# The stores of the attention's results move from SyncE's queue to ScalarE's

## The chip, the cores and the metric

The kernel runs on one core of a Trainium2 chip. The metric is the device time of one execution in microseconds (us); lower is better. The times shown are the median of several runs with the lowest and the highest of them. The profile comes from one further execution, whose own time is given beside its span.

Names used below: TensorE (PE) does matmuls and transposes, VectorE (DVE) and ScalarE (ACT) work on tiles elementwise, GpSimd (POOL) copies, and SyncE (SP) issues DMAs. An engine runs its instructions in order. A DMA is started by an instruction on an engine's queue, which takes a few tenths of a microsecond there; the transfer then goes on by itself, and whoever needs its data waits on a semaphore. In the profile, "SPq" stands for such issuing rows on SP.

## What is computed

Block-sparse attention for 4 batches and 8 heads, with 768 positions of 64 elements, followed by an MLP over the 3072 tokens:

```python
scores = scale * np.matmul(q, k.transpose(0, 1, 3, 2))
mask = np.abs(blk_i - blk_j) <= window          # blocks of 32 positions, window 1
mask = mask | (blk_i == 0) | (blk_j == 0) | (blk_i == n_blocks - 1) | (blk_j == n_blocks - 1)
# and 3 sampled key blocks for each query block
scores = np.where(mask, scores, -1000000000.0)
attn = np.exp(scores - np.max(scores, axis=-1, keepdims=True))
attn = attn / (np.sum(attn, axis=-1, keepdims=True) + 1e-09)
x = np.matmul(attn, v)        # then transposed and reshaped to 3072 x 512
h = x @ w_in                  # 512 x 2048, weights in float64
g = s * np.maximum(h, 0.0) ** 2 + b
out = g @ w_out               # 2048 x 512
```

## The kernel before

The attention is cut into 52 *slots*. A slot is a tile of 128 rows of queries for a few heads of one batch; most (kind s) see a static stretch of keys and their own sampled blocks, and the first and last blocks of a sequence, which see all keys, are slots of kind d (dense) and h. A slot has four *units* (a d slot two), and each unit is one score tile of up to 128×352.

The way of a slot through the engines, with the lines by which the profile names the steps:

- SP loads what is needed: keys `kt` (L490), queries `qr` (L500), values `v` (L508, L511, L514), and with `gather_v` (L653) the sampled value blocks `vg`. A gather is twelve or so single DMAs whose addresses come out of registers, so each has a register instruction beside it. POOL copies the sampled keys into `kg` (L670).
- PE computes the scores against static keys (L710, dense L724) and sampled keys (L736).
- DVE adds the mask and finds the row maximum (`maximum`, L751, one per unit); ACT computes the exponentials (L763, one per unit, with the row sum).
- PE transposes the exponentials (L787, 12 per slot); the four results `pt` are copied out of PSUM half by DVE (L791) and half by ACT (L793).
- PE multiplies them with the values: L832 (dense L821, kind h L826) for static ones, L846 for the gathered `vg`.
- DVE divides by the row sums (`x_scale`, L852), PE transposes the result (`x_transpose`, L858), ACT copies it from PSUM to an SBUF tile `xst` (`x_copy`, L863), and a DMA stores `xst` to `xd` in device memory (`spill`, L875): 128 KB for 44 of the slots, 64 KB for the 8 of kind d.

On PE these steps are interleaved: transposes of slot i, L858 of slot i−1, scores of slot i+2, then the value products of slot i. Tiles rotate in pools: `xst` has 4 buffers, `vg` 2 (each serves two batches), `v` 4, `raw` 3.

The MLP reads `xd` back (`xload`, L359), splits it into high and low parts (L372, L374), and multiplies with `w_in` (L401–L403) and `w_out` (L440–L442, and products of sums, L1193). The float64 weights arrive as integer words (`load`, L57, tiles `raw_i` and `raw_o`) and are decoded by DVE and ACT in nine steps (L75–L85) that begin during the second half of the attention.

What sets the order: the steps of the attention, the decoding and the first MLP units are handed as operations to a planner (class `Plan`, L99). Each has an engine, a cost in ns, a due time and its dependences. The planner simulates the five engines, takes the earliest operation that can start, and breaks ties by due time; the result is the order in which instructions are written. The engines then run that order, held only by semaphores. For a DMA on SP the planner also counts eight in flight (`QUEUE`): SP is taken as held until the DMA eight places earlier has landed. After 30 MLP units the rest is written in a fixed order by hand (L1242 on).

A DMA signals its landing on one of eight semaphores, which are taken in turn over all DMAs of the program; one that gets a semaphore again waits first until the DMA that had it last has landed.

In a spill's operation, `u` is the slot's first unit, and `T["XA"]` and `T["SPP"]` are offsets of the due time, −12 and −14 units:

```python
ac = op("a", 280 if kind == "d" else 390, u + T["XA"], lambda i=i: x_copy(i), [tr], alloc=[("xst", i)], use=[("o", i)])
```

Of the kernel before, what the change touches and what calls it, by code (L numbers as in the profile page):

```python
# [98 lines left out]
class Plan:  # L99
# [15 lines left out]
    def op(self, eng, cost, prio, fn, deps=(), alloc=(), use=(), order=(), nbytes=0, cols=0, late=0.0):  # L115


        o = Plan.Op()
        o.cost, o.prio, o.fn, o.nbytes, o.cols, o.late = cost if isinstance(cost, dict) else {eng: cost}, prio, fn, nbytes, cols, late
        o.pick = isinstance(cost, dict)  # L120
        o.deps, o.order, o.alloc = [d for d in deps if d], [d for d in order if d], alloc
        o.end, o.seq = None, len(self.ops)
        for k in (*alloc, *use):
            self.users.setdefault(k, []).append(o)
        self.ops.append(o)
        return o
# [76 lines left out]
def kernel(  # L203
# [16 lines left out]
    nc = tc.nc  # L220
# [238 lines left out]
    with ExitStack() as es:  # L459
# [400 lines left out]
        def x_copy(i):  # L860
            tr = tr_of.pop(i)
            xst_of[i] = xp.tile([P, 2, P], F32, tag="xst", name=f"xst{i}", bufs=4)[:, :tr.shape[1], :]
            nc.scalar.copy(xst_of[i], tr)  # L863

        def spill(i):
            kind, b, t, x = slots[i]
            hf, o = divmod(t * P, HALF)
            xst = xst_of.pop(i)
            if kind == "s":
                to = xd[b, hf, :, o // P, 2 * x:2 * x + 2]  # L870
            else:
                d0 = D * (kind == "d")
                to = xd[b, hf, :, o // P, 2 * x:2 * x + 2 * xst.shape[1], d0:d0 + D].rearrange("p (x a) q -> p x a q", a=2)
                xst = xst.rearrange("p x (a q) -> p x a q", a=2)
            nc.sync.dma_start(out=to, in_=xst)  # L875


        plan = Plan({"kraw": RB, "qr": QB, "v": 4, "kg": 4, "vg": 2, "B": NBANK,
# [2 lines left out]
        op = plan.op  # L881
        first, last = {}, {}
        for n, (i, j) in enumerate(units):
            kind, b, t, x = slots[i]
# [69 lines left out]
        spills, tensor, lqs = {}, {}, {}  # L954
# [3 lines left out]
        for i, (kind, b, t, x) in enumerate(slots):  # L958
            u, full, cost, col = unit_of[i], kind == "s", costs[kind], cols[kind]
            nu, ng, nk = (2, 2, 2) if kind == "d" else (4, 1, 2)  # L960
            qk = slots[i][:3]
            if qk not in lqs:
                for par in range(2):
                    pq = lqs[qk] = op("s", 450, u - T["QL"] + 0.1 * par, lambda qk=qk, par=par: load_q(qk, par), alloc=[] if par else [("qr", qk)],
                                      use=[("qr", qk)] if par else [], order=[pq], nbytes=131e3)
# [16 lines left out]
            if gd:  # L982
                o = op("p", cost[1], u, lambda i=i: scores_sampled(i), cols=col[1], deps=gd,
                       use=[("qr", qk), *gu, *(("B", ("s", *y)) for y in s_of)])
# [31 lines left out]
            if gd:  # L1016
                o = op("p", cost[4], u, lambda i=i: av_sampled(i), cols=col[4], deps=gvs[(b, t)],
                       use=[("o", i), ("vg", (b // 2, t)), *(("pt", (u + j, 0)) for j in range(nu))])
                a_ops.append(o)
            xc = op("v", 300 if kind == "d" else 430, u + T["XA"], lambda i=i: x_scale(i), [a_ops[-1], o_rc], alloc=[("xss", i)], use=[("o", i), ("rc", i)])  # L1020
            tr = op("p", 160 if kind == "d" else 230, u, lambda i=i: x_transpose(i), [xc], cols=256 if kind == "d" else 512, use=[("xss", i), ("o", i)])
            ac = op("a", 280 if kind == "d" else 390, u + T["XA"], lambda i=i: x_copy(i), [tr], alloc=[("xst", i)], use=[("o", i)])
            spills[i] = op("s", 450, u + T["SPP"], lambda i=i: spill(i), [ac], use=[("xst", i)], nbytes=66e3 if kind == "d" else 131e3)
            tensor[i] = s_ops, t_ops, a_ops, tr
        line = tensor[0][0] + tensor[1][0]
        for i in range(len(slots)):
# [20 lines left out]
        for g in range(2):  # L1047
            for c2 in range(2):
# [8 lines left out]
                for c in (2 * c2, 2 * c2 + 1):  # L1057
# [3 lines left out]
                                               use=[key], order=o_x)  # L1061
                    xs_ops[(g, c, 1)] = op("v", 450, N + T["XP"] + g * 16, lambda g=g, c=c: xsplit(g, c, 1), [h], use=[key], alloc=xkey[1], order=[xs_ops[(g, 0, 1)]] if c else [])
        wdone = {}
        for k, (which, f) in enumerate((w[0], int(w[1:])) for w in T["WL"].split()):
# [4 lines left out]
            for m, (eng, fn, needs) in enumerate(st):  # L1069
# [20 lines left out]
                if which == "i" and m == 6:  # L1090
                    if f % 4 == 0:
                        alloc = [(f"kt{f // 4}", ("win", f // 4))]
                    else:
                        order = [wdone[("i", f - 1, 6)]]
                mine[m] = wdone[(which, f, m)] = op(eng, cost[m], N + T["WP"] + T["WS"] * k + 0.3 * m, fn, deps, alloc=alloc, order=order,
                                                    use=[raw] * (m in (0, 1, 2, 3, 6)) + [wp] * (m > 0) + [("vg", f"wos{f // 4}")] * (which == "o" and m == 6 and f < 8 and f != 4))
# [35 lines left out]
    u = {n: (wos["x"], xsum["u"])[k // 2][:, k % 2 * HALF:(k % 2 + 1) * HALF] for k, n in enumerate(("m1", "u1", "u2", "u3"))}  # L1132
# [51 lines left out]
    def product(n):  # L1184
        a, x = PAIRS[n]
        to = bank(turns[0] % 2, f"m{turns[0]}")[:, :HALF]
        turns[0] += 1
        xl_of = (lambda c: tcn(xop[x][:, HX:])[:, :, c, :]) if x not in xsum else (lambda c: xop[x][:, HX + c * HALF:HX + (c + 1) * HALF])
        for c in range(2):
            wh, wl = (wop[a][:, (2 * k + c) * P:(2 * k + c + 1) * P] for k in range(2))  # L1190
            xh, xl = xop[x][:, c * HALF:(c + 1) * HALF], xl_of(c)
            for k, (w_, x_) in enumerate(((wh, xh), (wh, xl), (wl, xh))):
                nc.tensor.matmul(to, w_, x_, start=(c == 0 and k == 0), stop=(c == 1 and k == 2))  # L1193
        return to
# [3 lines left out]
    def take(gf, in0, in1, how):  # L1198

        i = made[0]  # L1200
        made[0] += 1
        t = htile(i % 2)
        vec.tensor_tensor(out=t, in0=in0, in1=in1, op=how)
        vec.scalar_tensor_tensor(out=t, in0=t, scalar=0.0, in1=t, op0=ALU.max, op1=ALU.mult)  # L1204
        fifo.append((i, gf))
        return i
# [61 lines left out]
    for s in range(S0, B):  # L1268
        a, b = 2 * s, 2 * s + 1
        for p in range(NFC // 2):  # L1270
            for n in (1, 2, 6, 7, 5, 3, 4):
                to = product(n)
                i = None
# [4 lines left out]
                elif n == 2:  # L1278
                    i = take((a, p), to, u["m1"], ALU.add)
# [4 lines left out]
                elif n == 5:  # L1284
                    i = take((b, p + 8), to, u["u2"], ALU.add)
                    vec.tensor_tensor(out=u["u3"], in0=to, in1=u["u1"], op=ALU.add)  # L1286
                elif n == 3:
                    i = take((b, p), to, u["u3"], ALU.add)
                else:
                    i = take((a, p + 8), u["u2"], to, ALU.subtract)  # L1290
# [93 lines left out]
```

## Time and profile before

| | |
|---|---|
| median of 3 runs | 809.02 us (808.52 to 810.49) |
| profiled execution, its own time | 807.75 us |
| its span | 805.9 us |
| mean granted TensorE clock | 0.991 |
| busy: PE, DVE, ACT, POOL | 785.6, 565.8, 492.8, 140.9 us |
| moved by DMA | 95.60 MB, 119 GB/s on average |
| spills (L875) | 52, issued from 30.0 to 281.0 us |

The attention takes about the first 281 us, the rest is MLP. The page's slices show the same division: forty equal stretches of the span, in each the tenths for which an engine was busy.

```profile
PE   7899998999999999999999999999999999999997
...
ACT  3577776787887787777763333457445457544542
```

A row of the timeline reads: start in us from the span's start, duration in us, engine, line, operation, result and operands, number of instructions merged; in brackets the idle time of the engine just before, and what ended it.

### The profile page before, as it was taken

Reading aid. Unit: us, or ns where it says so; the run is one execution under the profiler, and the core shown is the slowest. Engines: PE = TensorE matmul, PEld = TensorE weight load, DVE = VectorE, ACT = ScalarE, POOL = GpSimd, SP = SyncE. Lnnn points to the kernel's source line nnn. Section 1 sums busy time; section 2 is a strip of 40 time slices with the busy share of each in tenths; the row PEclk is TensorE's granted clock in tenths of the full one; section 3 lists DMA queues with packets and bytes.
Section 4 is the critical chain, followed back from the end, with each engine's and each line's share of the span. In section 5 each row is a group of like instructions: output and inputs, shape, how many; then the busy total and the mean of one; then the engine's idle time right before and its main releaser. Section 6 shows DMA issues by size and latency. Waiting matters only on the chain.

```text
span 805.9 us, 21894 instructions
## 1 busy us (share of the span) xinstructions
PE 785.6 (97%) x8400; PEld 681.6 (85%) x8400; DVE 565.8 (70%) x1445; ACT 492.8 (61%) x1175; POOL 140.9 (17%) x372
## 2 busy tenths in 40 slices
PE   7899998999999999999999999999999999999997
PEld 5588886888887889999899999998889988999996
DVE  5577776888887998999743333388768769766662
ACT  3577776787887787777763333457445457544542
POOL 5422142222400000000000000002223222322321
PEclk8899999999999999999999999999999999999999
DMA  9999798876777533334221010412200012000002
GB/s 252 248 228 325 223 255 247 242 213 206 210 211 248 145 107 108 107 125 131 86 99 39 27 40 27 149 45 88 86 1 7 0 40 90 10 0 1 1 1 78
DMA packets 86071, 95.60 MB, mean 119 GB/s; under 512 B 11344, under 2 KB 64976, under 8 KB 85968
## 3 DMA queue, kind: packets, MB, share of 16 engines
q1 hardware_dynamic: 85968, 94.21, 39.0%
q8 instruction: 66, 1.08, 0.6%
q14 instruction: 37, 0.30, 0.1%
HBM read 77.41 MB, written 12.58 MB: 112 GB/s over the span
## 4 chain that ended last, share of the span: by engine, by line
PE 87%; DVE 5%; DMA 4%; ACT 2%; SPq 1%; issue 1%; DVEq 0%; ACTq 0%
PE m L1193 14%; PE o L441 10%; PE o L442 10%; PE o L440 10%; PE t L787 9%; PE s L710 5%; PE xs L832 5%; PE h L403 5%; PE h L401 5%; PE h L402 5%; PE xs L846 3%; PE s L736 3%; DMA kt<-in_k_seq_dram 2%; PE s L724 1%; PE xs L858 1%; PE xs L821 1%
## 5 line engine op out<-in xcount | busy, mean ns | idle before, releaser
L419 POOL TENSOR_TENSOR hid<-hid,hid 128x384 fp32r<-128x384 f32 x64 | 68.9, 1077 | 512.5 <-ACT hid L1211 510.4
L763 ACT ACTIVATE ptile<-ptile,nm 128x352 f32<-128x352 f32 (+2 forms) x208 | 121.1, 584 | 35.8 <-DVE nm L751 35.5
L1210 ACT ACTIVATE hid<-hid,sb_b,sb_s 128x384 f32<-128x384 f32 x64 | 45.4, 709 | 110.6 <-DVE hid L1204 110.6
L751 DVE CUSTOM_DVE_ANT_0 ptile<-s,ms 128x352 f32<-128x352 f32 x160 | 74.3, 521 | 30.1 <-PE s L736 29.9
L670 POOL COPY kg<-kt 128x128 f32 x264 | 63.9, 302 | 135.1 <-PE s L736 122.6
L401 PE MATMUL h<-x,win 128*128 128x384 f32 x256 | 86.4, 337 | 0.0
L403 PE MATMUL h<-x,win 128*128 128x384 f32 x256 | 86.3, 337 | 0.0
L402 PE MATMUL h<-x,win 128*128 128x384 f32 x256 | 85.9, 336 | 0.0
L787 PE MATMUL t<-ident,ptile 128*128 128x128 f32 x608 | 80.2, 281 | 1.8 <-ACT ptile L763 1.3
L410 DVE SCALAR_TENSOR_TENSOR hid<-hid,sb_s 128x384 f32<-128x384 f32 x64 | 39.4, 616 | 53.9 <-ACT hid L406 53.7
L441 PE MATMUL o<-wout,hid 128*128 128x512 f32 x192 | 76.0, 396 | 0.6 <-DVE wout L85 0.6
L442 PE MATMUL o<-woutr,hid 128*128 128x512 f32 x192 | 75.9, 395 | 0.0
L442 PE MATMUL o<-wout,hid 128*128 128x512 f32 x192 | 75.9, 395 | 0.0
L441 PE MATMUL o<-woutr,hid 128*128 128x512 f32 x192 | 75.8, 395 | 0.0
L440 PE MATMUL o<-wout,hid 128*128 128x512 f32 x192 | 74.8, 390 | 0.0
L440 PE MATMUL o<-woutr,hid 128*128 128x512 f32 x192 | 74.6, 389 | 0.0
L787 PEld LDWEIGHTS t<-ident,ptile 128*128 128x128 f32 x608 | 66.6, 142 | 8.7 <-issue 2.2
L406 ACT ACTIVATE hid<-h 128x384 f32<-128x384 f32 x64 | 31.4, 491 | 69.6 <-PE h L403 69.1
L791 DVE COPY pt<-t 128x384 f32<-128x384 f32 (+1 forms) x104 | 56.3, 543 | 8.3 <-PE t L787 6.6
L419 DVE TENSOR_TENSOR hid<-hid,hid 128x384 fp32r<-128x384 f32 x64 | 35.6, 556 | 34.3 <-ACT hid L415 34.1
L1193 PE MATMUL m<-xT,wop 128*128 128x384 f32 x288 | 58.5, 337 | 0.7 <-DVE sum L1286 0.7
L793 ACT COPY pt<-t 128x384 f32<-128x384 f32 (+1 forms) x104 | 48.1, 474 | 15.3 <-PE t L787 15.2
(169 smaller groups left out, 1660.1 us busy)
## 6 DMA issues: line engine op xcount, KB each, us to landing
vg<-in_v_dram SPq DMA_DIRECT2D x136, 128.0 KB, 3.6
v<-in_v_sta_dram SPq DMA_DIRECT2D x40, 256.0 KB, 4.2
kt<-in_k_seq_dram SPq DMA_DIRECT2D x16, 544.0 KB, 8.0
raw_i<-in_w_in_dram SPq DMA_DIRECT2D x16, 512.0 KB, 4.4
raw_o<-in_w_out_dram SPq DMA_DIRECT2D x16, 512.0 KB, 3.2
v<-in_v_dram SPq DMA_DIRECT2D x16, 384.0 KB, 5.0
xd<-xst SPq DMA_DIRECT2D x44, 128.0 KB, 3.7
out_dram<-ob SPq DMA_DIRECT2D x20, 256.0 KB, 2.4
```

What stands on the lines that cost most here:

```text
L401: nc.tensor.matmul(ph, wh, xh, start=(c == 0), stop=False)
L402: nc.tensor.matmul(ph, wh, xl, start=False, stop=False)
L403: nc.tensor.matmul(ph, wl, xh, start=False, stop=(c == NCC - 1))
L419: (eng or nc.vector).tensor_tensor(out=htile(5 + i % 3), in0=t, in1=gh.bitcast(F32), op=ALU.subtract)
L440: nc.tensor.matmul(acc, gh[:, tsl], wout(f, 0), start=first, stop=False)
L441: nc.tensor.matmul(acc, gh[:, tsl], wout(f, 1), start=False, stop=False)
L442: nc.tensor.matmul(acc, gl[:, tsl], wout(f, 0), start=False, stop=last)
L670: nc.gpsimd.tensor_copy(kg[:, m], kts[b][:, :, bass.ds(box["js"][m], BLK)])
L751: nc.vector.tensor_tensor_reduce(out=pt[:, :w], in0=sps.pop((n, g))[:, :w], in1=msk, scale=-scale, scalar=FMAX if g == 0 else nm[:, 0:1], ...
L763: nc.scalar.activation(pt[:, :w], pt[:, :w], AF.Exp, bias=nms[n][:, last:last + 1], scale=-1.0, accum_out=dns[i][:, g, j:j + 1])
L787: nc.tensor.transpose(tp[:, c, :], src[:, c * P:(c + 1) * P], ident)
L1193: nc.tensor.matmul(to, w_, x_, start=(c == 0 and k == 0), stop=(c == 1 and k == 2))
```

## The change

The DMA that stores `xst` is issued by ScalarE, whose own copy made the tile, and not by SyncE. In the planner the operation moves with it, from engine s to engine a: charged 100 ns, not 450, due right behind the copy (u − 11.9, not u − 14), and no longer counted among SP's eight in flight. What it depends on stays the same.

```diff
@@ spill
                 xst = xst.rearrange("p x (a q) -> p x a q", a=2)
-            nc.sync.dma_start(out=to, in_=xst)
+            nc.scalar.dma_start(out=to, in_=xst)
@@ the operations of a slot
             ac = op("a", 280 if kind == "d" else 390, u + T["XA"], lambda i=i: x_copy(i), [tr], alloc=[("xst", i)], use=[("o", i)])
-            spills[i] = op("s", 450, u + T["SPP"], lambda i=i: spill(i), [ac], use=[("xst", i)], nbytes=66e3 if kind == "d" else 131e3)
+            spills[i] = op("a", 100, u + T["XA"] + 0.1, lambda i=i: spill(i), [ac], use=[("xst", i)], nbytes=66e3 if kind == "d" else 131e3)
```

Line numbers are the same in both kernels. As the planner sees other costs, some neighbouring operations change places too. PE's order stays the same through the attention, but for one group of three MLP matmuls (L401–L403) that stood ahead of the last dense value products and now comes later.

The first place is SP's queue in the second quarter of the attention, from a load of edge values to the load of the indices (L646) behind which twelve gathers into one `vg` buffer stand. In the names, the number behind a tile tells its turn in the program. Before:

```order
L511 DMA v_0_2666<-in_v_edge_dram 128x2x256
L57 DMA raw_i_2672<-in_w_in_dram 128x4x256
L875 DMA xd<-xst_2670 128x256
L500 DMA qr_4s<-in_q_dup_dram 64x4x128 x2
L511 DMA v_0_2770<-in_v_edge_dram 128x2x256
L875 DMA xd<-xst_2821 128x256
L500 DMA qr_0s<-in_q_dup_dram 64x4x128 x2
L514 DMA v_0_2923<-in_v_sta_dram 128x512
L875 DMA xd<-xst_2983 128x256
L500 DMA qr_0s<-in_q_dup_dram 64x4x128 x2
L514 DMA v_0_3074<-in_v_sta_dram 128x512
L646 TENSOR_LOAD vidx
```

And now:

```order
L511 DMA v_0_2682<-in_v_edge_dram 128x2x256
L500 DMA qr_4s<-in_q_dup_dram 64x4x128 x2
L511 DMA v_0_2770<-in_v_edge_dram 128x2x256
L500 DMA qr_0s<-in_q_dup_dram 64x4x128 x2
L514 DMA v_0_2923<-in_v_sta_dram 128x512
L500 DMA qr_0s<-in_q_dup_dram 64x4x128 x2
L514 DMA v_0_3074<-in_v_sta_dram 128x512
L646 TENSOR_LOAD vidx
```

Three spills are gone from between the loads, and the weight load `raw_i` that stood here has moved ahead, two loads of values earlier.

The second place is ACT's queue around the copy of one slot's result. Before:

```order
L763 ACTIVATE ptile_80,dn_2335<-ptile_80,nm_2355 128x352
L793 COPY pt_0_2383<-t_0_2364 128x384
L863 COPY xst_2391<-xs_2314 128x256
L793 COPY pt_0_2399<-t_0_2375 128x384
L763 ACTIVATE ptile_81,dn_2335<-ptile_81,nm_2362 128x352
```

And now:

```order
L763 ACTIVATE ptile_84,dn_2216<-ptile_84,nm_2236 128x352
L793 COPY pt_0_2274<-t_0_2251 128x384
L863 COPY xst_2282<-xs_2177 128x256
L875 DMA xd<-xst_2282 128x256
L793 COPY pt_0_2294<-t_0_2265 128x384
L763 ACTIVATE ptile_85,dn_2216<-ptile_85,nm_2247 128x352
```

The spill stands directly behind its copy and ahead of the second copy of `pt`; the rest of a slot's row stays as it was.

The third place is the load of the sixth `raw_i` and its first decode step, late in the attention. On SP before:

```order
L514 DMA v_0_6064<-in_v_sta_dram 128x512
L875 DMA xd<-xst_6099 128x256
L57 DMA raw_i_6147<-in_w_in_dram 128x4x256
L514 DMA v_0_6172<-in_v_sta_dram 128x512
L875 DMA xd<-xst_6216 128x256
L514 DMA v_0_6282<-in_v_sta_dram 128x512
```

And now:

```order
L514 DMA v_0_6058<-in_v_sta_dram 128x512
L514 DMA v_0_6166<-in_v_sta_dram 128x512
L57 DMA raw_i_6253<-in_w_in_dram 128x4x256
L514 DMA v_0_6278<-in_v_sta_dram 128x512
L359 DMA wout_6288<-xd 128x3x256 x2
```

The weight load has moved behind one more load of values. On DVE the decode step that reads it (L75) stood before the four maxima of a slot (`ptile_78` to `ptile_81`), here the first two of them:

```order
L774 TENSOR_SCALAR rc_6329<-dn_6174 128x4
L775 RECIPROCAL rc_6329<-rc_6329 128x4
L374 TENSOR_TENSOR x_1_6105<-xraw_1_4807,x_0_5921 128x384
L75 TENSOR_SCALAR wkhp_3257<-raw_i_6147 128x512
L751 ISA ptile_78,nm_6365<-s_6315,ms 128x352
L751 ISA nm_6365 128x1
L751 ISA ptile_79,nm_6392<-s_6317,ms 128x352
```

and now stands behind the last of these four and the steps that follow them:

```order
L751 ISA ptile_81,nm_6399<-s_6324,ms 128x352
L751 ISA nm_6399 128x1
L852 TENSOR_TENSOR xss_6409<-xs_6350,rc_6317 128x256
L791 COPY pt_0_6416<-t_0_6394 128x384
L791 COPY pt_0_6426<-t_0_6405 128x384
L774 TENSOR_SCALAR rc_6434<-dn_6280 128x4
L775 RECIPROCAL rc_6434<-rc_6434 128x4
L75 TENSOR_SCALAR wkhp_3259<-raw_i_6253 128x512
L77 TENSOR_SCALAR wklp_3281<-raw_i_6253 128x512
L751 ISA ptile_82,nm_6468<-s_6420,ms 128x352
```

So the decode step has moved back by one slot.

## The prediction

> **What bounds the kernel now.** First the busy times on the profile's page:
>
> ```profile
> PE 785.6 (97%) x8400; PEld 681.6 (85%) x8400; DVE 565.8 (70%) x1445; ACT 492.8 (61%) x1175; POOL 140.9 (17%) x372
> ```
>
> TensorE is busy 97% of 805.9 us, so an edit that touches no matmul can win only where TensorE waits. The view of busy times by stretches (us; each engine busy, times in brackets; granted clock; share of the DMA engines; GB/s) finds those places:
>
> ```profile
> core 0: us, PE busy (x) PEld busy (x) DVE busy (x) ACT busy (x) POOL busy (x), PEclk, DMA share, GB/s
> 76.00:112.00 36.00, 35.78 (x876) 29.14 (x874) 25.66 (x92) 26.27 (x80) 5.90 (x25) 1.00 0.86 243
> 116.50:135.00 18.50, 18.50 (x470) 14.99 (x464) 14.86 (x60) 14.91 (x47) 8.71 (x36) 1.00 0.87 242
> 135.00:145.00 10.00, 6.78 (x116) 5.63 (x114) 4.13 (x14) 4.07 (x13) 0.48 (x3) 0.83 0.84 233
> 145.00:240.00 95.00, 95.00 (x2320) 78.14 (x2318) 81.05 (x284) 77.29 (x235) 22.86 (x95) 1.00 0.75 216
> 240.00:250.00 10.00, 8.74 (x198) 7.12 (x200) 7.04 (x27) 6.33 (x20) 0.00 (x0) 1.00 0.89 285
> 297.00:800.00 503.00, 502.11 (x2495) 451.36 (x2496) 338.23 (x667) 276.87 (x543) 68.91 (x64) 1.00 0.16 54
> ```
>
> From 145 to 240 us there is nothing to win: 95.00 of 95. From 297 us to the end TensorE is busy 502.11 of 503, with few transfers, so an attention part that ends earlier by x ends the kernel earlier by about x. Two holes remain: 135–145, where the granted clock falls to 0.83 as well, and 240–250.
>
> **Stall A, 135 us.** TensorE's timeline there (start, us, engine, line, idle before it and what ended it):
>
> ```profile
> 130.71 1.53 PE L787 MATMUL t<-ident,ptile 128*128 128x128 f32 x12
> 132.07 0.38 PE L858 MATMUL xs<-ident,xss 128*128 128x128 f32 x2
> 135.02 0.30 PE L846 MATMUL xs<-vg,pt 96*32 96x64 f32 x4
> 136.04 0.27 PE L846 MATMUL xs<-vg,pt 96*32 96x64 f32 x2 [0.72 <-DMA vg<-in_v_dram]
> 138.82 0.97 PE L846 MATMUL xs<-vg,pt 96*32 96x64 f32 x26 [2.50 <-DMA vg<-in_v_dram]
> 139.72 2.77 PE L787 MATMUL t<-ident,ptile 128*128 128x128 f32 x12
> 142.33 0.38 PE L858 MATMUL xs<-ident,xss 128*128 128x128 f32 x2
> ```
>
> Two pieces of the chain of waits:
>
> ```profile
> 121.88 0.58 PE xs L846 x32
> ...
> 135.46 3.28 DMA vg<-in_v_dram
> ```
>
> Between one x_transpose (L858) and the next lie 142.33 − 132.07 = 10.26 us. An ordinary slot takes 4.90 (the rows at 201.55 and 206.45 below), so 5.36 us are lost: 0.72 + 2.50 waiting for gathered rows, 2.77 − 1.53 = 1.24 on transposes at the lower clock that follows the pause, the rest in the slowed L846. Both buffers of vg rotate; this one came free when the last L846 of an earlier slot ended, 121.88 + 0.58 = 122.46. Yet its first gather goes out at 127.96 and its last at 135.46. SP's timeline says why (ahead of it, ACT's copy that made the tile of the first spill shown; both are the 17th of their line):
>
> ```profile
> 110.20 0.37 ACT L863 COPY xst<-xs 128x256 f32<-128x256 f32 x1 [0.78 <-PE xs L858]
> 118.68 0.45 SPq L875 DMA_DIRECT2D xd<-xst  x1
> 121.21 0.42 SPq L875 DMA_DIRECT2D xd<-xst  x1
> 124.54 0.38 SPq L875 DMA_DIRECT2D xd<-xst  x1
> 127.96 1.44 SPq L653 DMA_DIRECT2D vg<-in_v_dram  x3
> 129.83 0.35 SPq L875 DMA_DIRECT2D xd<-xst  x1
> 130.37 4.40 SPq L653 DMA_DIRECT2D vg<-in_v_dram  x8
> 134.88 0.39 SPq L875 DMA_DIRECT2D xd<-xst  x1
> 135.46 0.36 SPq L653 DMA_DIRECT2D vg<-in_v_dram  x1
> ```
>
> Twelve gathers at about half a microsecond each (4.40 / 8 = 0.55) stand in one line with everything else, and five spills stand ahead of the last. That first spill left 118.68 − 110.57 = 8.1 us after its tile was ready: SP was behind already. This is a queue limited by its own issue time.
>
> **Stall B, 241 us.** A piece of the chain, then rows of TensorE, VectorE and SP in the timeline:
>
> ```profile
> 240.88 5.93 DMA raw_i<-in_w_in_dram
> ```
>
> ```profile
> 242.91 0.38 PE L858 MATMUL xs<-ident,xss 128*128 128x128 f32 x2
> 246.84 0.43 DVE L75 TENSOR_SCALAR wkhp<-raw_i 128x512 int32<-128x512 int32 x1 [2.69 <-DMA raw_i<-in_w_in_dram]
> 249.43 0.44 PE L858 MATMUL xs<-ident,xss 128*128 128x128 f32 x2 [1.06 <-DVE xss L852]
> 241.36 0.64 SPq L514 DMA_DIRECT2D v<-in_v_sta_dram  x1
> ```
>
> A decode step (L75) stands in VectorE's order ahead of four row maxima (L751) and waits for its weights; the slot takes 249.43 − 242.91 = 6.52, so 1.6 us are lost.
>
> **The change, part by part.** *Taken from SP:* the spills (duration in ns, least, median and most; then landing).
>
> ```profile
> L875 SPq DMA_DIRECT2D xd<-xst x52: 326/372/1782, 30.0 to 281.0; - x52
> DMA to landing us min/median/max: 1.6/3.7/8.5
> ```
>
> The last two of the five spills ahead of the last gather hold SP, with the gap behind them, for 130.37 − 129.83 = 0.54 and 135.46 − 134.88 = 0.58 us; five at some 0.55 are 2.7. The row of all spills gives one per (281.0 − 30.0) / 51 = 4.9 us, so about seven more stood in 76–112, while SP was falling behind; that is another 3.9. TensorE wants the first of these gathers at 135.02 and the last some 0.6 later; it landed at 135.46 + 3.28 = 138.74. So some 3.2 us are needed and up to 6.6 are freed, with the buffer free 5.5 us before its first issue. I take stall A as gone: **−5.3**. The bounds: 5.36 at most; at least 2.4. That floor supposes the DMA engines themselves limit the loads: their share is 0.87 over 18.5 us, which at a share of 1.0 would be 16.1 us, and 2.4 us less of waiting.
>
> *Stall B:* in the new order L57 stands behind that L514, and L75 behind the four maxima that it held up, one slot later. Even issued no earlier than L514 was (241.36), with the same 5.93, the words land at 247.3; VectorE reaches L75 at about 246.84 − 2.69 + 4.90 = 249.05. **−1.6**, bounds −1.6 and 0. The load before this one moves further back, from the 43rd to the 47th v load of SP's order, with no room that I could find: +0.3, bounds 0 and +0.5.
>
> *Put on ACT:* two ordinary slots and, from a third, how closely ACT runs on:
>
> ```profile
> 201.55 0.37 ACT L863 COPY xst<-xs 128x256 f32<-128x256 f32 x1 [0.87 <-PE xs L858]
> 206.45 0.37 ACT L863 COPY xst<-xs 128x256 f32<-128x256 f32 x1 [0.39 <-PE xs L858]
> 243.33 0.37 ACT L863 COPY xst<-xs 128x256 f32<-128x256 f32 x1 [0.34 <-PE xs L858]
> 243.60 0.48 ACT L793 COPY pt<-t 128x384 f32<-128x384 f32 x1
> 244.78 1.15 PE L832 MATMUL xs<-v,pt 128*64 128x64 f32 x32
> ```
>
> L793 begins 0.10 before the copy's end at 243.70. The spill must wait for that end, and then takes the 0.37 that it takes on SP: L793 begins about 0.37 + 0.10 + 0.05 (issue) = 0.52 later, at 244.12, and ends at 244.60. L832, which needs pt, begins at 244.78: covered. The exponentials behind it move by the same 0.52. What absorbs it is ACT's idle time: from 145 to 240 us ACT is busy 77.29 of 95, so 17.7 us lie free in 95 / 4.90 = 19.4 slots, 0.91 each; 0.39 remains. No issue on ACT is in this trace, so its price is bounded by SP's fastest and slowest, 0.33 and 1.78; I take the median, to which nearly all rows are near. Slots with less than the mean free, and the short dense ones, may give a little: **+0.6** (0 to +1.5).
>
> The spills' consumers are reads of the MLP stage, and a spill that leaves right behind its copy can only land earlier; xst has four buffers. No one waits for it.
>
> *The order:* the planner no longer sees the spill in SP's line. Three MLP matmuls (L401–L403) leave a gap at 276.8:
>
> ```profile
> 276.80 0.42 PE L401 MATMUL h<-x,win 128*128 128x384 f32 x1
> 277.73 1.62 PE L821 MATMUL xs<-v,pt 128*64 128x64 f32 x48 [0.16 <-ACT xst L863]
> ```
>
> The three take until about 277.57, some 0.5 beyond the transpose in front; done later, they cost **+0.5**, the wait for the copy (0.9 in all) being left unfilled.
>
> **Sum:** −5.3 − 1.6 + 0.3 + 0.6 + 0.5 = −5.5. From the profiled execution, 807.75 (its span of 805.9 and 1.85 around it), that is 802.25; this execution was 1.27 under the median of the runs shown, and from that median, 809.02, it is 803.5.
>
> The Trainium skill's page "DMA: Bandwidth & Descriptors", section "Issuing engines are not separate DMA queues", speaks against the change: DMAs of several issuers share the same 16 DMA engines, and a second issuer saves only sequencer time, "usually small". By that rule the sum would be near that of the first rival below, 807.7. SP's rows between 118.68 and 135.46 show it back to back at a DMA share of 0.87, so here the sequencer's time is what is short, and I keep the sum.
>
> **Rivals.**
>
> *The issuers take turns* (about 807.7). If issuing from ACT holds up an issue on SP for as long as a spill took there, SP's line advances no faster, stall A stays, and only the new places count: 809.02 − 1.6 + 0.3 = 807.7, within the same band if ACT and the filler add their 1.1 (808.8). For it: nothing in the trace shows two issuers at once. Against it: SP's cost per row differs by kind (0.37 for a spill, 0.55 for a gather with its register work), so part at least is the sequencer's own. The Trainium skill's "Perfetto Trace Analysis", section "DMA Instruction — HWDGE (DVE, Sync)", says a descriptor generator is locked for exclusive use while it is set up; no row here shows whether ACT and SP would share one.
>
> *Half of A* (about 806). The DMA engines set the pace: −2.4 in place of −5.3, so 803.5 + 2.9 = 806.4. For it, shares of 0.86 and 0.87; against it, 285 GB/s in 240–250 beside 242 here.
>
> *Slower: ACT becomes the bound* (about 816). A spill waits on ACT for two semaphores, that of ACT's copies and one of the eight that rotate over the DMAs of both queues, hence for the landing of the DMA eight places back. Behind it stand that slot's L793 and four exponentials, for which PE's transposes (L787) wait. If the spill holds ACT for 1.43 us, by that wait or by dear issues like SP's 1.78, then 1.43 − 0.91 = 0.52 go beyond the idle time in each of the (281 − 145) / 4.90 = 28 slots from 145 us on: +14.4, against the −7 or so won, about 816. It cancels the gain where the spill holds ACT for 0.91 + 7 / 28 = 1.16. Against it: spills land in a median 3.7 us, and eight gathers alone take 4.40 to issue, so the DMA eight places back has mostly landed.
>
> **How the numbers follow.** Forecast 803.5: 0.65, its own range 801 to 806. Half of A: 0.11, about as often under as over the bound. Issuers in turns: 0.12. ACT bound: 0.12. A measurement of this kernel can tell about 0.3%, 2.4 us: faster is under 806.6, slower over 811.4. Faster: 0.65 + 0.06 = 0.71; same: 0.05 + 0.12 = 0.17; slower 0.12. The range 801 to 810 takes in the first three cases and leaves out ACT's.
>
> **What would show it.** Right: no wait of L846 for vg over 0.5 us, no drop of the clock near 139, 4.90 from slot to slot through 145 us; L75 with no wait before it; spills of 0.3–0.4 on ACT's queue, issued within 0.1 of the copy's end; PE still busy 95 of 95 in mid-attention. Wrong: gathers that leave SP as late as before (turns), gathers that leave early and land late (DMA bound), L787 waiting for ACT in many slots (ACT bound), or a new wait of a decode step where raw_i loads moved back.

## The result, and the profile after

| | before | after |
|---|---|---|
| median of 6 runs each | 809.23 us (808.52 to 810.49) | 841.05 us (838.62 to 846.5) |
| ratio | | 1.0402 (95% interval 1.0363 to 1.0442) |
| span of the profiled execution, granted clock | 805.9 us, 0.991 | 838.1 us, 0.977 |

The change makes the kernel 4% slower; 0.7% faster was forecast. The page of the changed kernel gives the busy times:

```profile
PE 795.8 (95%) x8400; PEld 691.1 (82%) x8400; DVE 567.0 (68%) x1445; ACT 496.0 (59%) x1175; POOL 140.4 (17%) x372
```

ACT computes what it did (496.0 us for 492.8), and PE is busy 10 us longer for the same 8400 matmuls, at a lower granted clock: 0.977, not 0.991. It falls behind the longer pauses: after one of 5.2 us at 85 us, twelve transposes (L787) take 2.82 us where 1.53 is usual. The other 22 of the 32 us are time in which PE stands still. The view of stretches (columns as before) shows where:

```profile
33.00:62.00 29.00, 24.62 (x488) 21.05 (x485) 15.90 (x57) 16.35 (x50) 10.21 (x45) 0.85 0.66 175
62.00:76.00 14.00, 14.00 (x351) 11.56 (x349) 10.10 (x38) 10.43 (x32) 3.89 (x17) 1.00 0.61 173
76.00:112.00 36.00, 28.54 (x614) 23.73 (x603) 19.20 (x69) 19.58 (x59) 5.83 (x24) 0.91 0.75 244
112.00:145.00 33.00, 30.67 (x769) 25.28 (x767) 21.77 (x82) 22.96 (x70) 11.56 (x48) 1.00 0.74 214
145.00:170.00 25.00, 19.82 (x422) 15.94 (x399) 15.41 (x55) 14.09 (x43) 5.79 (x24) 0.86 0.76 213
170.00:240.00 70.00, 70.00 (x1743) 57.87 (x1746) 58.95 (x208) 56.48 (x170) 20.33 (x84) 1.00 0.69 201
240.00:300.00 60.00, 55.48 (x1177) 43.65 (x1166) 45.57 (x159) 44.06 (x132) 0.00 (x0) 0.97 0.74 214
330.00:830.00 500.00, 499.09 (x2478) 448.70 (x2478) 334.98 (x660) 274.07 (x538) 68.83 (x64) 1.00 0.16 53
```

From 76 to 112 us PE stood still for 7.5 us, where it had been busy 35.78 of 36. Yet from 170 to 240 it is busy 70.00 of 70, with every spill of that time on ACT. So what loses is not simply the time that a spill takes there. The copies into `xst` date the slots. The row of all copies, before and then after:

```profile
L863 ACT COPY xst<-xs x52: 249/373/378, 25.9 to 280.7; 128x256 f32<-128x256 f32 x44, 128x128 f32<-128x128 f32 x8
```

```profile
L863 ACT COPY xst<-xs x52: 248/372/382, 25.5 to 308.7; 128x256 f32<-128x256 f32 x44, 128x128 f32<-128x128 f32 x8
```

The last copy begins at 308.7, not at 280.7: 28.0 of the 32.2 us of span are lost in the attention, the rest just behind it, at the front of the MLP.

What PE waits for in the changed kernel (us in total, times, longest):

```profile
PE xs L832 <- DMA v<-in_v_sta_dram: 10.5, 5, 5.2
PE xs L846 <- DMA vg<-in_v_dram: 8.7, 5, 2.7
PE s L724 <- DMA kt<-in_k_seq_dram: 3.6, 2, 2.6
PE xs L821 <- DMA v<-in_v_dram: 3.0, 1, 3.0
```

Loads are late, now those of v as well. And why SP, relieved of 52 issues, issues them late, its own waits tell:

```profile
SPq L653 <- DMA xd<-xst: 36.5, 18, 5.2
SPq L500 <- DMA xd<-xst: 13.5, 5, 4.8
SPq L514 <- DMA xd<-xst: 4.7, 2, 2.6
SPq L490 <- DMA xd<-xst: 3.9, 1, 3.9
SPq L359 <- DMA xd<-xst: 3.7, 2, 2.3
```

In 28 places, for 62.3 us, SP waits for the landing of a *spill*, a DMA that it doesn't issue and whose data it doesn't need (but for the reads at L359). The program has the reason. In these rows of its order the semaphores that an instruction waits for stand in brackets; first a spill on ACT, then part of SP's queue:

```
ACT  L863 COPY xst_685<-xs_542 128x128 [waits PE_49]
ACT  L875 DMA xd<-xst_685 128x2x64 [waits DMAHW2_49,Activation_49]
...
SP   L653 DMA vg_0_380<-in_v_dram 32x2x512 [waits DMAHW1_49]
SP   L653 DMA vg_0_380<-in_v_dram 32x2x512 [waits DMAHW2_49]
SP   L653 DMA vg_0_380<-in_v_dram 32x2x512 [waits DMAHW3_49]
SP   L508 DMA v_0_606<-in_v_dram 128x6x128 [waits DMAHW4_49,PE_49]
```

The eight semaphores go round over the DMAs of both queues. The second gather shown is eight DMAs behind the spill in the program, gets its semaphore, and must wait until the spill has landed. On the chip (timelines of ACT, of SP, a piece of the chain, and PE's timeline):

```profile
37.08 0.25 ACT L863 COPY xst<-xs 128x128 f32<-128x128 f32 x1
37.37 0.37 ACTq L875 DMA_DIRECT2D xd<-xst  x1
```

```profile
39.03 0.82 SPq L653 DMA_DIRECT2D vg<-in_v_dram  x2
39.94 0.40 SPq L508 DMA_DIRECT2D v<-in_v_dram  x1
```

```profile
39.94 5.95 DMA v<-in_v_dram
```

```profile
46.03 2.83 PE L821 MATMUL xs<-v,pt 128*64 128x64 f32 x48 [2.98 <-DMA v<-in_v_dram]
```

The spill, issued at 37.37, lands 1.6 us later, at 39.01; the gather leaves at 39.03, after a wait of 5.2 us, the longest of the list. Behind it stands a load of v (L508), for which PE then waits until 46.0. So SP can stand at most seven DMAs past a spill that has not landed, and a spill lands only after PE, DVE and ACT have finished a slot.

### The profile page after: what moved, and what is told of

Read it like the earlier page. It is cut to its first block, busy times and chain, and to the rows that moved or that the text cites. A ratio compares the mean times of both kernels' runs of the same rounds, so it can differ in the third digit from the quotient of the medians.

```text
span 838.1 us, 21838 instructions
## 1 busy us (share of the span) xinstructions
PE 795.8 (95%) x8400; PEld 691.1 (82%) x8400; DVE 567.0 (68%) x1445; ACT 496.0 (59%) x1175; POOL 140.4 (17%) x372
## 3 DMA queue, kind: packets, MB, share of 16 engines
q10 hardware_dynamic: 10048, 6.29, 2.5%
## 4 chain that ended last, share of the span: by engine, by line
PE 82%; DMA 8%; DVE 3%; ACT 3%; SPq 2%; issue 1%; ACTq 0%; DVEq 0%
PE m L1193 13%; PE o L441 10%; PE o L442 10%; PE o L440 10%; PE t L787 8%; PE h L401 5%; PE h L403 5%; PE h L402 5%; PE xs L832 5%; PE s L710 4%; PE xs L846 3%; DMA v<-in_v_sta_dram 3%; DMA kt<-in_k_seq_dram 2%; PE s L736 2%; PE xs L821 2%
## 5 line engine op out<-in xcount | busy, mean ns | idle before, releaser
L787 PE MATMUL t<-ident,ptile 128*128 128x128 f32 x608 | 83.7, 290 | 2.9 <-ACT ptile L763 2.9
L401 PE MATMUL h<-x,win 128*128 128x384 f32 x256 | 86.3, 337 | 0.0
L403 PE MATMUL h<-x,win 128*128 128x384 f32 x256 | 86.3, 337 | 0.0
L793 ACT COPY pt<-t 128x384 f32<-128x384 f32 (+1 forms) x104 | 47.8, 469 | 51.3 <-PE t L787 28.7
L787 PEld LDWEIGHTS t<-ident,ptile 128*128 128x128 f32 x608 | 70.2, 148 | 9.0 <-ACT ptile L763 4.1
```

The source lines that it names most:

```text
L401: nc.tensor.matmul(ph, wh, xh, start=(c == 0), stop=False)
L403: nc.tensor.matmul(ph, wl, xh, start=False, stop=(c == NCC - 1))
L787: nc.tensor.transpose(tp[:, c, :], src[:, c * P:(c + 1) * P], ident)
```

## The experiments

Three theories: **A**, the shared semaphores just described; **B**, the planner's new order of the loads; **C**, ACT's time.

**Only the engine.** The plan stays that of before, with the spill planned on SP:

```diff
-            nc.sync.dma_start(out=to, in_=xst)
+            nc.scalar.dma_start(out=to, in_=xst)
```

> Only the issuing engine is changed; the planner still plans the spill on SP, so all loads keep the order of before. Theory A (shared semaphores: a DMA on SP waits for the landing of the DMA eight places back in the program, which may now be a spill that ACT has not issued yet): SP waits for xd landings again, but less than in the changed kernel, since the spill stands further back in the program; 805 to 825 us. Theory B (the planner's new order of the loads, K in one burst ahead of V, is what loses): the loss is gone, 802 to 809. Theory C (the issue time on ACT loses): about 840.

Measured: 847.79 us, ratio 1.048 (1.0446 to 1.0514). B falls: the old order loses even more. The size is C's and not A's, but SP's waits for xd landings are there, 77.6 us of them, the largest:

```profile
SPq L653 <- DMA xd<-xst: 41.4, 16, 5.0
SPq L514 <- DMA xd<-xst: 13.6, 6, 4.1
```

I had thought that the spill's place further back in the program would ease the coupling; it doesn't. A and C stay open after this run.

**Only the plan.** The order of the changed kernel, SP issues:

```diff
-            nc.scalar.dma_start(out=to, in_=xst)
+            nc.sync.dma_start(out=to, in_=xst)
```

> Only the planner's line is changed: the order is that of the changed kernel word for word, but SP issues the spill at its place. A: SP no longer waits for a spill's landing, but waits in its own row for the copy that makes the tile; part of the loss stays, 815 to 835, with SP's waits on ACT xst in place of waits on xd landings. B: the whole loss stays, 838 to 845. C: the loss is gone, 803 to 812.

Measured: 810.81 us, ratio 1.0029 (1.0006 to 1.0052). B falls a second time: the new order by itself costs 0.3%. The number is the one that C expected; A had put the loss from SP's waiting for copies too high. In SP's waits stands, in place of the landings:

```profile
SPq L875 <- ACT xst L863: 15.3, 11, 2.4
```

**The spill on GpSimd**, whose DMAs take none of the eight semaphores (these go round over SP's and ACT's alone), with the changed plan:

```diff
-            nc.scalar.dma_start(out=to, in_=xst)
+            nc.gpsimd.dma_start(out=to, in_=xst)
```

> The changed kernel's plan, but GpSimd issues the spill. Its DMAs take none of the eight semaphores that SP's DMAs rotate over. A: SP's waits for xd landings vanish and the loss with them, 802 to 812. B: 838 to 845. C: 802 to 810, as ACT is free of the issue; A and C part by SP's waits in the trace and by the runs of ACT's issue time in e1.

Measured: 809.18 us, ratio 1.0006 (0.9982 to 1.003). SP waits for no landing of xd, and the loss is gone. Stalls A and B of the prediction are gone too. ACT's copies around the two places in this run:

```profile
137.43 0.37 ACT L863 COPY xst<-xs 128x256 f32<-128x256 f32 x1 [0.22 <-PE xs L858]
142.33 0.37 ACT L863 COPY xst<-xs 128x256 f32<-128x256 f32 x1 [1.03 <-PE xs L858]
...
243.06 0.37 ACT L863 COPY xst<-xs 128x256 f32<-128x256 f32 x1 [1.03 <-PE xs L858]
247.96 0.37 ACT L863 COPY xst<-xs 128x256 f32<-128x256 f32 x1 [0.34 <-PE xs L858]
```

Both slots take 4.90 us. Why the time is still only that of before is told below. A and C both expected this number.

**Let the planner count ACT's spills** among the eight in flight that hold SP:

```diff
-                if e == "s":
-                    sent.append(dma + 850.0)
-                    free[e] = max(free[e], sent[-self.QUEUE])
+                sent.append(dma + 850.0)
+                free["s"] = max(free["s"], sent[-self.QUEUE])
```

> The changed kernel, with the planner counting the spill on ACT among the eight DMAs in flight that hold SP, as the semaphores do. A: the order fits the chip again, SP's waits for xd landings fall by more than half, 805 to 825. B: the order of the loads changes in an unknown way; if K still goes out in one burst ahead of V, 835 to 845. C: about 840.

Measured: 845.56 us, ratio 1.0449 (1.0407 to 1.0491): a miss for A. SP's waits for xd landings grow to 73.5 us over five lines, the largest (this kernel's lines are numbered one lower)

```profile
SPq L652 <- DMA xd<-xst: 43.8, 18, 4.7
```

A planner that knows the rule doesn't lift it. Why it doesn't even find an order that suits the rule was not settled.

**ACT held longer, no semaphore taken.** The run on GpSimd, and ACT copies `xst` onto itself behind each copy:

```diff
             xst = xst_of.pop(i)
+            nc.scalar.copy(xst, xst)
```

> GpSimd issues the spill as in the run before, with the changed plan, and ACT copies xst onto itself once more, 0.37 us behind each copy, so that ACT is held about as long as by a spill. C (ACT's time is what loses): 835 to 845. A: ACT's idle time takes it, 808 to 813.

Measured: 809.4 us, ratio 0.9996 (0.9974 to 1.0019), like the run without it. The extra copy takes 0.40 us, about as long as a spill on ACT:

```profile
202.09 0.37 ACT L863 COPY xst<-xs 128x256 f32<-128x256 f32 x1 [0.80 <-PE xs L858]
202.50 0.40 ACT L869 COPY xst<-xst 128x256 f32<-128x256 f32 x1
202.81 0.47 ACT L793 COPY pt<-t 128x384 f32<-128x384 f32 x1
```

The second copy of `pt` begins 0.72 us behind the start of the first copy into `xst`, where the spill made it 0.80 and without either it is 0.27. C falls: ACT has this time to spare.

**A semaphore taken, almost no data.** The run on GpSimd, and ACT issues a DMA of 256 bytes from the same tile to a scratch tensor of its own:

```diff
             xst = xst_of.pop(i)
+            nc.scalar.dma_start(out=xnote[i:i + 1], in_=xst[0:1, 0, :D])
```

> GpSimd issues the spill as before, and ACT issues a further DMA of 256 bytes from the same tile at the spill's place of the changed kernel, so that the place in the rotation of the eight semaphores is taken again, with almost no data behind it. A: the loss is back, somewhat smaller since a small DMA lands sooner, 820 to 840, and SP waits for landings of xnote. C: as the run with the longer ACT copy. If the contention of the spills' data with the loads were what loses: 808 to 813.

Measured: 830.28 us, ratio 1.0235 (1.019 to 1.028): 21 us lost to 52 DMAs of 13 KB together. SP's waits name them, here the two largest (lines numbered one higher):

```profile
SPq L654 <- DMA xnote<-xst: 30.1, 11, 5.5
SPq L501 <- DMA xnote<-xst: 13.2, 6, 3.3
```

Neither ACT's time (0.2 us per issue here) nor the spills' data is what loses; the place in the rotation is. This run decides for A. The other 11 of the 32 us were not taken apart; A had expected part of the loss.

**Fewer DMAs in the rotation.** The changed kernel, spills on ACT, with the loads of the queries on GpSimd:

```diff
-            nc.sync.dma_start(out=qraw[key][rows], ...)
+            nc.gpsimd.dma_start(out=qraw[key][rows], ...)
```

> The changed kernel, spills on ACT, but GpSimd issues the loads of the queries (L500), so that they too take none of the eight semaphores. A: SP can stand at most seven DMAs past a spill that has not landed; with about two DMAs fewer per slot in the rotation, seven reach further ahead in time, so a third to two thirds of the 32 us come back: 818 to 832 us, and SP waits less than 62 us for landings of xd. If what loses is not the number of DMAs between a spill and its successor on the same semaphore, the time stays at 838 to 846.

Measured: 828.85 us, ratio 1.0214 (1.0185 to 1.0243): some 12 of the 32 us come back, as A expects (by the two ratios to the kernel before, 15). But SP's waits for xd landings did not fall; over five lines they are 103.5 us, the largest

```profile
SPq L653 <- DMA xd<-xst: 62.4, 23, 6.9
```

SP, with less to issue, simply waits more. So the sum of its waits is no measure of the loss, only the waits behind which a load comes too late for PE are. The changed kernel shows it too, where between 170 and 240 us SP waits 17.9 us for such landings, over four lines, and PE never pauses. The run also takes 56 issues off SP, so by itself it does not part the rotation from that relief.

**GpSimd with the plan of before**, one line changed:

```diff
-            nc.sync.dma_start(out=to, in_=xst)
+            nc.gpsimd.dma_start(out=to, in_=xst)
```

> The kernel before with one line changed: GpSimd issues the spill, the plan stays. A (shared semaphores): SP is relieved of 52 issues and tied to nothing; the stalls at 135 and 241 us shrink, and what the new order cost elsewhere (about 1.4 us at the start and 2.7 us at the front of the MLP in the run with the changed plan) stays away: 801 to 805 us. Rival (SP gains nothing, whoever is relieved; the stalls went only through the new order): 808 to 811.

Measured: 806.68 us, ratio 0.9958 (0.9936 to 0.998), a little above A's range and under the rival's; the profiled span is 804.3. It is the smallest edit that beats both kernels, by 0.4% over the one before.

**GpSimd, and the planner knows it** (GpSimd issues; the planner's line against that of the changed kernel):

```diff
-            spills[i] = op("a", 100, u + T["XA"] + 0.1, ...)
+            spills[i] = op("g", 560, u + T["XA"] + 0.1, ...)
```

> GpSimd issues the spill and the planner knows it: an operation of 560 ns on engine g, due right behind the copy. A: like the run with GpSimd and the changed plan, 803 to 811, by what the order of the loads and of the decoding comes to; SP waits for no landing of xd before the end of the attention.

Measured: 806.42 us, ratio 0.9958 (0.9937 to 0.9979), not to be told from the last. No line of SP's waits names xd.

## Why the prediction was wrong

- **The step that failed** is "No one waits for it." The prediction looked for waits on a spill only among the readers of its data, and gave such waits no term in the sum. But SP's DMA eight places behind a spill waits for that spill: in 28 places, 62.3 us in all. With these waits gone and the plan unchanged (the run on GpSimd), the 32 us are gone. The rival on ACT had named the rule, that a DMA waits "for the landing of the DMA eight places back" over "the DMAs of both queues", and then asked only whether *ACT* would wait for SP. ACT's list has one such wait, 1.3 us (L793 for xd). So the place was wrong, and so was the reason against it, that "the DMA eight places back has mostly landed": it holds for SP's loads, which leave at their turn, and not for a spill, which leaves when a slot is done. Before, a spill stood in SP's own row, so SP could not run ahead of it: at times it waited there for the copy itself, and at others the tile had long been ready (8.1 us in the rows that the prediction quotes). Its waits before:

```profile
SPq L875 <- ACT xst L863: 21.0, 12, 3.5
```

 That the rival's 816 lay on the right side was luck: the runs do not show its mechanism.
- **Stall A, −5.3:** right, once SP is really free. Between the 22nd and the 23rd copy lies this slot; on GpSimd it takes 142.33 − 137.43 = 4.90 in place of 10.26, so −5.36, and with the plan of before 4.90 as well (135.89 to 140.79), so the floor of 2.4, set by the DMA engines, was not seen. In the changed kernel SP was not free, and the slot grew to 165.17 − 153.08 = 12.09, with PE waiting 5.0 us in it for `vg`:

```profile
153.08 0.36 ACT L863 COPY xst<-xs 128x256 f32<-128x256 f32 x1
165.17 0.37 ACT L863 COPY xst<-xs 128x256 f32<-128x256 f32 x1 [7.89 <-PE xs L858]
```

 Two readings behind the term were too simple. SP was not back to back there before the change: its own waits between 118.6 and 135.9 us come to 4.5 us, the longest (1.4) for L787. And not all of the stall needs SP's relief: in the run with only the plan, SP issuing, the slot takes 144.20 − 137.66 = 6.54.
- **Stall B, −1.6:** right, in the changed kernel too: from the 44th copy to the 45th it takes 277.20 − 272.30 = 4.90, though L75 then waits 1.7 us one slot later. On GpSimd it is 247.96 − 243.06 = 4.90. The forecast credited the new places of L57 and L75, and with these alone, SP issuing, the slot takes 4.90 too; SP's relief does it as well, for the slot is as short on GpSimd with the plan of before (242.66 to 247.56).
- **ACT, +0.6:** the mechanism right, the size 0. A spill takes 0.35 at 108.50, 0.04 after the copy's end, and L793 begins 108.89 − 108.09 = 0.80 after the copy's start where it was 0.27: 0.53 later, for 0.52 forecast. PE lost nothing by it (70.00 of 70 us, and the run with the longer copy).

```profile
108.09 0.37 ACT L863 COPY xst<-xs 128x256 f32<-128x256 f32 x1 [0.40 <-PE xs L858]
108.50 0.35 ACTq L875 DMA_DIRECT2D xd<-xst  x1
108.51 0.88 SPq L653 DMA_DIRECT2D vg<-in_v_dram  x2
108.89 0.48 ACT L793 COPY pt<-t 128x384 f32<-128x384 f32 x1 [0.42 <-ACT xst L863]
```

- **Issuers take turns:** these rows speak against it. ACT and SP issue within 0.01 us of each other, and neither takes as long as both would. Over the whole run 18 of SP's 136 gather issues overlap with a spill's issue on ACT; their median is 0.33 us, that of the others 0.32.
- **The order, +0.3 and +0.5:** too small. With the changed plan on GpSimd the last copy begins at 278.8, 1.9 us sooner than before, and the span is 0.8 longer: 2.7 us are lost between. PE there waits for decoded weights, in the changed kernel just as in this run,

```profile
PE o L441 <- DVE wout L85: 1.3, 2, 0.7
PE o L440 <- DVE wout L83: 0.9, 1, 0.9
```

 where before it waited 0.6: 1.6 of the 2.7. The three moved matmuls take about 0.5, as forecast; the rest, some 0.6, was not taken apart. With the plan of before on GpSimd the copies end at 278.4, 2.3 sooner, and the span is 1.6 shorter.
- **What the sum lacked even so:** stalls A and B are 7.0 us, and the attention on GpSimd ends only 1.9 or 2.3 sooner. Some 5 us are lost anew, with the changed plan nearly all of them ahead of stall A. There the copy ahead of it begins at 137.43, where it was 132.49: 4.9 us later. 1.4 of that are there by the second copy, with a granted clock of 0.80 from 30 to 45 us where it was 0.90. Nearly all of the rest lies in slots with pauses in which PE waits for nothing that the profile shows ("issue"), the longest:

```profile
114.67 0.33 PE L787 MATMUL t<-ident,ptile 128*128 128x128 f32 x1 [2.03 <-issue]
```

 There are 3.7 us of these between 60 and 135 us in that run, and 0.6 before. The forecast of the new order missed this too: with the same plan and SP issuing, the same copy begins at 137.66, and on GpSimd with the plan of before at 135.89. What causes the pauses is not shown.
- The Trainium skill's "DMA: Bandwidth & Descriptors", section "Issuing engines are not separate DMA queues", was set aside in the prediction with too light a hand: it says that a further issuer saves only sequencer time, usually little. The best runs agree with it, 806.4 and 806.7 for 809.1.

## What to carry to other kernels

Ask of a DMA that moves to another queue not only what it will wait for, but who waits for it: where queues share a small set of completion semaphores in turn, a DMA with a late source holds back the queue that had been running ahead, even when it is small: 256 bytes per slot cost 21 us here. A program's list of waits shows this without a run, row by row, at the instruction eight DMAs behind. And a queue that is short of issue time is better relieved by an issuer outside that rotation, here GpSimd, than by one inside it; in this kernel that brought 0.4%.

## What the runs showed of the hardware

The two queues that share the semaphores show up apart in the page's list of queues of the changed kernel, the spills' 6.29 MB on one of their own:

```profile
q1 hardware_dynamic: 75920, 87.92, 34.6%
q10 hardware_dynamic: 10048, 6.29, 2.5%
```

An issue on GpSimd took 0.54 us in the median, on ACT 0.33, on SP 0.37; a spill landed after a median of 4.0 or 3.6 us from GpSimd (changed plan, plan of before), 3.3 from ACT and 3.7 from SP. PE's "issue" pauses do not simply go with dense transfers: from 100 to 118 us the run on GpSimd with the changed plan has the one of 2.03 us at a DMA share of 1.01 (full), and that with the plan of before keeps PE busy 18.00 of 18 us at 1.02.
